# A depthwise convolution ahead of a SwiGLU block: two of the early blocks pass from the token-major to the channel-major convolution, and the convolution's taps are dealt out anew

## The chip, the core and the metric

The program runs on one core of one Trainium2 chip. The core has five engines that each work through their own queue in order: TensorE (PE in the profile, its weight loads PEld), VectorE (DVE), ScalarE (ACT), GpSimd (POOL) and SyncE (SP, which here only issues DMAs). They wait for one another by semaphores. The metric is the device time of one execution in microseconds (us); the median of three executions of the kernel before is 771.72 us (771.16 to 772.36).

## What is computed

`x` has 8 x 4096 tokens of 192 channels. Eight heads of 24 channels each have 7 taps, softmax-normalised; every channel is convolved causally along the sequence with its head's taps. The result goes through a gated feed-forward block of width 1536.

```python
w = weight - np.max(weight, axis=-1, keepdims=True)
w = np.exp(w)
w = w / (np.sum(w, axis=-1, keepdims=True) + 1e-09)
x_pad = np.concatenate([np.zeros((B, pad, D)), x], axis=1)      # pad = 6
out = np.einsum('hk,bskhg->bshg', w, x_unf)                     # 7 shifted copies of x
...
g = x @ w_gate                                                  # 192 -> 1536
silu = g * (1.0 / (1.0 + np.exp(-g)))
val = x @ w_val
return (silu * val @ w_out)                                     # 1536 -> 192
```

## The kernel before

**Blocks and steps.** The 32768 tokens are cut into 64 blocks of 512. A block goes through 12 chunks of 128 of the 1536 hidden columns, so there are 768 steps; step n is chunk j = n mod 12 of block b = n div 12. `gate_val(n)` (line 734) issues, for one step, six matmuls: three slices of 64 channels for the gate and, in the other 64 rows of the array, three for the value, in turn. ScalarE then makes `sig` (silu of the gate) and VectorE `h` = `sig` x value. Gate and value each have three PSUM banks, so the matmuls of step n+3 wait until `sig` and `h` of step n have read theirs.

**Down matmuls.** Behind every third step stands one of four `slot`s: 24 matmuls that multiply six chunks of `h` with the output weights, one half of the rows at a time, into two accumulators (`down`, line 759). In the steady order these are k = 1 behind chunk 7, 2 behind chunk 10, 3 behind chunk 1 of the next block and 4 behind its chunk 4; the last also copies the sums out (ScalarE one half, VectorE the other) and has SP store them. Block 0 has its slots behind steps 9, 12, 15 and 17 (lines 864 to 866). Where a slot changes which half of the rows writes which bank (`swap`), its first matmul is made to wait for a silu (`after`).

**Two ways to the convolved block.** The feed-forward needs each block channel-major, as three tiles `xc[b]` of 128 x 512.

- *Token-major, for the first blocks.* TensorE convolves windows of tokens with a band matrix: `early` for blocks 0 and 1, and `early_pair` (line 379) for blocks 2 and 3 at step 19 and 4 and 5 at step 27: 64 small matmuls into gate and value banks, which ScalarE and VectorE copy to `tme`. From there a block either is turned by TensorE (`eturn`: blocks 0, 1, 2) or goes through DRAM: SP writes it out (`eout`, 4 DMAs) and reads it back by three DMA transposes (`efetch`: blocks 3, 4, 5). The inputs `xp` of the pairs are loaded at the start by GpSimd's DMAs and doubled by SP's (`twice`).
- *Channel-major, for the rest.* Four blocks make a unit; unit 1 here holds blocks 6 and 7 alone (`first_of`). GpSimd's DMA casts the tokens of a unit to fp16 in DRAM (`cast_x`), SP's DMA transposes bring them channel-major into SBUF (`turn_x`, four per two blocks) and a copy joins the last 64 channels of both blocks (`join_x`). Two blocks then are three jobs: a "block" job for 128 channels of each and a "pair" job for the remaining 64 of both. A job (`conv_job`, line 580) has 7 taps: ScalarE multiplies the first into `total` (fp32) and two more into `part` tiles, VectorE adds two taps into `total` (line 618, `tap * x + total`), GpSimd adds the `part`s, and multiplies (line 608, `piece`) and adds (line 593) the last two. All GpSimd's work of a job is issued after VectorE's and ScalarE's taps. `place` (line 653) then has SP move halves of the results into the other two tiles of each block, four DMAs.

**The order.** Each engine's order is the order of issue in the program. `pooled_work(n, j)` (line 708) deals out the taps: behind chunks 1, 7 and 10 one VectorE tap each and one ScalarE tap (two behind chunk 10 of even blocks); one more ScalarE tap stands ahead of the slot of chunk 4. `plan`, filled by `planned(v)` (line 678), holds at which step a unit's cast, transposes and jobs are issued. A block is handed over (`place`) once its two jobs are issued, 14 steps later or 16 steps ahead of its use.

Of the kernel before, what the change touches and what calls it, by code (L numbers as in the profile page):

```python
# [10 lines left out]
def kernel(  # L11
# [172 lines left out]
    xp = {}  # L184
    for e in (2, 4):
        xp[e] = cpool.tile([P, 4 * EG, D], fp16, tag="xp", name="xp")
        for r in range(2):
            windows(xp[e], Q * r, (e + r) * TB, CO, 0, 4 * EG)
        twice(xp[e])

# [243 lines left out]
    def efetch(b):  # L434
        xc[b] = []
        for k in range(SL):
            t = cpool.tile([P, XW], fp16, tag=f"xc{k}", name=f"xc{k}", bufs=8)
            seq(
                nc.sync.dma_start_transpose(
                    out=t[:, 0:TB], in_=scre[b][0:TB, Q * k : Q * k + P]  # L440
                )
            )
            xc[b].append(t)

    def eturn(b, where, then=None):
        c, j = (2, EO) if b < 2 else (4, CO)
        tiles = [
            cpool.tile([P, XW], fp16, tag=f"xc{k}", name=f"xc{k}", bufs=8)
            for k in range(SL)
# [75 lines left out]

    def first_of(u):
        return HALF if u == 1 else 0

    def head_x(u):
        rows = XP + UT - first_of(u) * TB  # L530
        xs[u] = dpool.tile([rows, D], fp16, tag="xs", name="xs")
        if u % upb == 0:
            seq(
                nc.sync.dma_start(
                    out=xs[u].rearrange("t d -> (t d)")[0 : XP * D].rearrange(
                        "(a n) -> a n", n=P
                    ),
                    in_=fill[0 : XP * D // P, :],
                )
            )  # L540

    def cast_x(u):
        t0 = u * UT + first_of(u) * TB
        rows = XP + u * UT + UT - t0
        flat = xs[u].rearrange("t d -> (t d)")
        skip = XP if u % upb == 0 else 0
        n = (rows - skip) * D // P
        seq(
            nc.gpsimd.dma_start(  # L549
                out=flat[skip * D : rows * D].rearrange("(a n) -> a n", n=n),  # L550
                in_=bass.AP(
                    tensor=x_flat.tensor,
                    offset=(t0 - XP + skip) * D,
                    ap=[[n, P], [1, n]],
                ),
                max_dma_last_dim=2048,
            )
        )

    def turn_x(u, i, at):  # L560
        r0 = TB * (i - first_of(u))
        rows = xs[u][r0 : r0 + TB + XP]
        tiles = (x01, x12)[at // Q]
        tag = f"x{at // Q}"
        t = cpool.tile([P, TB + XP], fp16, tag=tag, name=tag, bufs=8)
        seq(nc.sync.dma_start_transpose(out=t, in_=rows[:, at : at + P]))
        tiles[u, i] = t
# [4 lines left out]
    FIRST, ON_DVE = 0, (1, 2)  # L572
    SHARES = ((3, 4), (5, 6)), ((3, 4), (5, 6)), ((3, 4), (5, 6))
    act_steps = []
# [5 lines left out]
    def conv_job(u, what, i):  # L580
        index = n_jobs[0]
        n_jobs[0] += 1
        on_act, on_pool = SHARES[index % len(SHARES)]
        job = {"dve": len(ON_DVE), "act": len(on_act), "parts": []}
        at = XP - pad
# [3 lines left out]

        def add(part, k):  # L590
            total = job["total"]
            seq(
                nc.gpsimd.tensor_tensor(  # L593
                    job["dst"] if k == K - 1 else total, total, part, op=ALU.add
                )
            )

        def proceed():
            if job["dve"]:
                return  # L600
            while job["parts"]:
                add(*job["parts"].pop(0))
            if job["act"]:
                return
            for k in on_pool:
                part = cpool.tile([P, TB], fp32, tag="piece", name="piece", bufs=2)
                seq(
                    nc.gpsimd.tensor_scalar(  # L608
                        part, shifted(k), scalar1=job["tap"][:, k : k + 1],
                        scalar2=1.0, op0=ALU.mult, op1=ALU.mult,  # L610
                    )
                )
                add(part, k)
            finished[u, what, i] = step_now[0]

# [10 lines left out]
        def act_step(k):  # L626
# [12 lines left out]
            else:  # L639
                part = cpool.tile([P, TB], fp32, tag="part", name="part", bufs=8)  # L640
                job["parts"].append((part, k))
            seq(
# [3 lines left out]
            )  # L646
            if k != FIRST:
                job["act"] -= 1
                proceed()

        act_steps.extend((index, lambda k=k: act_step(k)) for k in (FIRST, *on_act))

    def place(u, i):
        b = UB * u + i
        for k in (1, 2):
            xc[b].append(
                cpool.tile([P, XW], fp16, tag=f"pxc{k}", name=f"pxc{k}", bufs=4)
            )
        t0, t1, t2 = xc[b]
        y = y2[u, i // 2][Q * (i % 2) : Q * (i % 2) + Q, :]  # L660
        for dst, src in (
            (t1[0:Q, 0:TB], t0[Q:P, 0:TB]),
            (t1[Q:P, 0:TB], y),
            (t2[0:Q, 0:TB], y),
            (t2[Q:P, 0:TB], t0[0:Q, 0:TB]),
        ):
            seq(nc.sync.dma_start(out=dst, in_=src))

    plan = {}
    placing = []  # L670

    def queue_jobs(u):
        for i in range(first_of(u), UB, 2):
            for job in (("block", i), ("pair", i // 2), ("block", i + 1)):
                conv_job(u, *job)
        placing.extend((u, i) for i in range(first_of(u), UB))

    def planned(v):
        s0 = ustep * v
        turns = [  # L680
            turn
            for i in range(first_of(v), UB, 2)
            for turn in ((i, 0), (i, Q), (i + 1, Q), (i + 1, 0), (i // 2, None))
        ]
        if v == 1:
            head, cast, jobs = 10, 11, 27
            times = (20, 20, 20, 23, 23)
        elif v == 2:
            head, cast, jobs = 10, 12, 40
            times = (32, 33, 34, 35, 37, 38, 39, 40, 41, 43)  # L690
        elif v == 3:
            head, cast, jobs = 56, 56, 56
            times = range(66, 86, 2)
        else:
            head = cast = s0 - (115 if v > 4 else 100)
            jobs = s0 - 89
            first = s0 - (95 if v > 4 else 87)
            times = range(first, first + 20, 2)
        plan.setdefault(head, []).append(lambda: head_x(v))
        plan.setdefault(cast, []).append(lambda: cast_x(v))  # L700
        for m, turn in enumerate(turns):
            def todo(i=turn[0], at=turn[1]):
                join_x(v, i) if at is None else turn_x(v, i, at)

            plan.setdefault(times[m], []).append(todo)
        plan.setdefault(jobs, []).append(lambda: queue_jobs(v))

    def pooled_work(n, j):
        step_now[0] = n
        if j != 4:  # L710
            ready = dve_steps[0][0] if dve_steps else None
            if j in (1, 7, 10) and ready is not None:
                dve_steps.pop(0)[1]()
            for _ in range(2 if j == 10 and n // NCH % 2 == 0 else 1):
                ahead = act_steps[0][0] if act_steps else n_jobs[0]
# [4 lines left out]
        while placing:  # L720
            u, i = placing[0]
            need = (u, "block", i), (u, "pair", i // 2)
            if not all(job in finished for job in need):
                break
            done = max(finished[job] for job in need)
            if n < max(done + 14, ustep * u + NCH * i - 16):
                break
            placing.pop(0)
            place(u, i)

# [71 lines left out]
    def slot(k, b, after=None):  # L802
# [11 lines left out]
        elif k == 3:  # L814
            down(b, [(False, G[2])], 1, after)
            down(b, [(False, G[3])], 1, None)
        else:
            down(b, [(True, G[2]), (True, G[3])], 0, after)
            o_sb = hpool.tile([P, SUBS, D], fp32, tag="o_sb", name="o_sb", bufs=3)
# [33 lines left out]
    make_band()  # L853
    for v in range(1, NU):
        planned(v)

    for n in range(n_steps):
# [4 lines left out]
        elif n == 8:  # L862
            eturn(1, (gate_bank, val_bank))
        elif n in (9, 12, 15, 17):
            k = {9: 1, 12: 2, 15: 3, 17: 4}[n]
            slot(k, 0, silu[n - 1 if k == 4 else n - 2])
        elif j % 3 == 1 and n > 18:
# [5 lines left out]
            slot(k, b - 1 if j < 7 else b, silu[n - 2])  # L873
        if n in (19, 27):
            early_pair(2 if n == 19 else 4)
        elif n == 20:
# [3 lines left out]
        elif n == 22:  # L880
            efetch(3)
        elif n in (28, 29):
            eout(n - 24)
        elif n in (30, 36):
            efetch(4 if n == 30 else 5)
        pooled_work(n, j)
# [44 lines left out]
```

## Time and profile before

| | |
|---|---|
| time, median of three (lowest, highest) | 771.72 us (771.16, 772.36) |
| the profiled execution: time, span of the trace | 771.32 us, 769.5 us |
| TensorE clock granted | 1.000 |
| VectorE / ScalarE / GpSimd busy | 702.5 / 649.1 / 637.8 us |
| VectorE `h` | 768 times, 682 ns mean |
| VectorE taps | 174 times, 1070 ns mean |
| VectorE `o_sb` copies | 63 times, 548 ns mean |
| ScalarE `sig`, taps | 596 ns, 714 ns mean |
| GpSimd products, adds | 918 ns, 1271 to 1419 ns mean |
| SP moves of 64 KB in `place` | 232 |
| first step's matmuls begin at | 8.84 us |

The profile shows one execution. "Busy" is the time in which an engine has an instruction under way, and a busy engine need not be the one that the end waits for: for that, the profile follows the last instruction back through whatever released it. A timeline line gives start and duration in us, the engine, the line of the kernel, the operation, the tiles it writes and reads with their shapes, how many like it follow one another, and in brackets the idle time before it with the instruction that ended it. Matmuls overlap, so two of them may each last 0.38 us and begin 0.04 us apart.

### The profile page before, as it was taken

The numbers are of one execution on the slowest core, as the hardware profiler recorded it, in microseconds if no ns is written. First come the engines' busy times: TensorE is split into PE (matmuls) and PEld (weight loads), VectorE is DVE, ScalarE is ACT, GpSimd is POOL, SyncE is SP. The second block draws the span as 40 slices with busy tenths as digits, with TensorE's granted clock in tenths as the row PEclk, the third lists the DMA queues.
The fourth block names the chain that finished last, engine by engine and source line by source line (L and its number), as shares of the span: only waits on it lengthen the run. The fifth ranks groups of instructions, "written<-read, shape, count | busy, mean of one in ns | idle before, by whom it ended". The sixth has DMA issues, their size and how long they took to land.

```text
span 769.5 us, 27729 instructions
## 1 busy us (share of the span) xinstructions
PE 763.0 (99%) x11041; PEld 616.1 (80%) x11041; DVE 702.5 (91%) x1048; ACT 649.1 (84%) x1114; POOL 637.8 (83%) x570
## 2 busy tenths in 40 slices
PE   8999999999999999999999999999999999999997
PEld 5878888888888888888888888888888888888886
DVE  7789999999999999999999999999999999999875
ACT  6688888888888888888888888888888888888764
POOL 8039899999989898998989989999899998889700
PEclk9999999999999999999999999999999999999999
DMA  9966646653536444456443545447454453121211
GB/s 143 198 115 122 154 80 149 128 88 84 123 81 124 106 85 108 99 95 119 92 102 89 100 111 108 92 82 118 92 120 101 82 116 92 53 70 37 71 56 43
DMA packets 145762, 77.52 MB, mean 101 GB/s; under 512 B 79976, under 2 KB 145504, under 8 KB 145632
## 3 DMA queue, kind: packets, MB, share of 16 engines
q1 hardware_dynamic: 126720, 61.05, 34.3%
q0 software_dynamic: 18912, 14.70, 13.8%
q8 instruction: 86, 1.41, 0.8%
q14 instruction: 44, 0.36, 0.2%
HBM read 29.39 MB, written 37.46 MB: 87 GB/s over the span
## 4 chain that ended last, share of the span: by engine, by line
PE 99%; ACT 0%; DVE 0%; issue 0%
PE val L743 51%; PE acc L769 33%; PE gate L743 14%; PE warm L837 0%; PE turn L457 0%; PE acc L790 0%; PE cv L394 0%; PE cv L350 0%; ACT tme L368 0%; DVE h L754 0%; ACT wide L308 0%; ACT o_sb L899 0%; PE taps L295 0%; DVE spread L275 0%; PE ctap L513 0%
## 5 line engine op out<-in xcount | busy, mean ns | idle before, releaser
L754 DVE TENSOR_TENSOR h<-sig,val 128x512 f16<-128x512 f16 x768 | 497.1, 682 | 59.4 <-PE gate L743 54.3
L752 ACT ACTIVATE sig<-gate 128x512 f16<-128x512 f32 x768 | 457.5, 596 | 107.9 <-PE gate L743 78.3
L743 PE MATMUL gate<-pxc,w 64*128 64x512 f16 x2088 | 488.0, 376 | 0.0
L743 PE MATMUL val<-pxc,w 64*128 64x512 f16 x2088 | 488.0, 376 | 0.0
L743 PEld LDWEIGHTS <-w 64*128 64x128 f16 x4608 | 360.1, 110 | 119.7 <-issue 0.7
L769 PE MATMUL acc<-wo,h 64*128 64x192 f16 x6096 | 336.7, 243 | 0.0
L769 PEld LDWEIGHTS <-h 64*128 64x128 f16 x6096 | 311.6, 94 | 21.4 <-ACT sig L752 0.4
L593 POOL TENSOR_TENSOR total<-total,part 128x512 f32<-128x512 f32 x174 | 221.8, 1275 | 73.8 <-DVE total L618 50.0
L618 DVE SCALAR_TENSOR_TENSOR total<-x,both_taps,total 128x512 f32<-128x512 f16 x174 | 186.2, 1070 | 0.0
L608 POOL TENSOR_SCALAR piece<-x,both_taps 128x512 f32<-128x512 f16 x174 | 159.7, 918 | 0.0
L593 POOL TENSOR_TENSOR total<-total,piece 128x512 f32<-128x512 f32 x87 | 123.5, 1419 | 7.3
L643 ACT ACTIVATE part<-x,both_taps 128x512 f32<-128x512 f16 x174 | 124.3, 714 | 0.0
L593 POOL TENSOR_TENSOR pxc<-total,piece 128x512 f16<-128x512 f32 x58 | 74.2, 1279 | 4.8
L643 ACT ACTIVATE total<-x,both_taps 128x512 f32<-128x512 f16 x87 | 62.1, 714 | 0.0
L743 PE MATMUL gate<-xc,w 64*128 64x512 f16 x216 | 51.4, 377 | 0.0
L743 PE MATMUL val<-xc,w 64*128 64x512 f16 x216 | 51.3, 376 | 0.0
L593 POOL TENSOR_TENSOR y<-total,piece 128x512 f16<-128x512 f32 x29 | 36.8, 1271 | 2.4
L821 DVE COPY o_sb<-acc 128x384 f32<-128x384 f32 x63 | 34.5, 548 | 0.0
L820 ACT COPY o_sb<-acc 128x384 f32<-128x384 f32 x63 | 29.6, 471 | 2.6 <-PE acc L769 2.6
L549 POOL DMA_DIRECT2D xs<-in_x_dram x15 | 11.7, 778 | 0.0
L837 PE MATMUL warm<-fill 128*128 128x512 f16 (+1 forms) x12 | 4.1, 500 | 1.0 <-DVE fill L90 1.0
L470 ACT COPY xc<-turn 128x520 f16<-128x520 f16 (+1 forms) x5 | 2.9, 588 | 1.0 <-PE turn L457 0.9
(66 smaller groups left out, 55.8 us busy)
## 6 DMA issues: line engine op xcount, KB each, us to landing
out_dram<-o_sb SPq DMA_DIRECT2D x63, 384.0 KB
pxc<-pxc SPq DMA_DIRECT2D x116, 64.0 KB
pxc<-y SPq DMA_DIRECT2D x116, 64.0 KB
xs<-in_x_dram POOLq DMA_DIRECT2D x7, 774.0 KB, 8.6
xs<-in_x_dram POOLq DMA_DIRECT2D x7, 768.0 KB, 7.0
x<-x SPq DMA_DIRECT2D x29, 66.0 KB
x<-xs SPq DMA_TRANSPOSE x116
xp<-in_x_dram POOLq DMA_DIRECT2D x4, 240.0 KB, 7.5
```

Source lines behind the costliest of these rows:

```text
L549: nc.gpsimd.dma_start(out=flat[skip * D : rows * D].rearrange("(a n) -> a n", n=n), in_=bass.AP(tensor=x_flat.tensor, offset=(t0 - XP + sk ...
L593: nc.gpsimd.tensor_tensor(job["dst"] if k == K - 1 else total, total, part, op=ALU.add)
L608: nc.gpsimd.tensor_scalar(part, shifted(k), scalar1=job["tap"][:, k : k + 1], scalar2=1.0, op0=ALU.mult, op1=ALU.mult,)
L618: nc.vector.scalar_tensor_tensor(job["total"], shifted(k), job["tap"][:, k : k + 1], job["total"], op0=ALU.mult, op1=ALU.add,)
L643: nc.scalar.activation(part, shifted(k), AF.Copy, scale=job["tap"][:, k : k + 1])
L743: nc.tensor.matmul(o, w16[m][p0 : p0 + Q, k, e::E], xc[b][k][p0 : p0 + Q, 0:TB], start=(k == 0), stop=(k == SL - 1),)
L752: silu[n] = seq(nc.scalar.activation(sg, g, AF.Silu)).ins
L754: seq(nc.vector.tensor_tensor(hj, sg, v, op=ALU.mult))
L769: nc.tensor.matmul(acc[b][bank][:, s, :], hj[p0 : p0 + Q, ts(2 * bank + s, P)], wo16[p0 : p0 + Q, j, :], start=(not second and j == 0 and ...
L820: seq(nc.scalar.copy(o_sb[:, 0:2, :], acc[b][0]))
L821: seq(nc.vector.tensor_copy(o_sb[:, 2:4, :], acc[b][1]))
L837: nc.tensor.matmul(warm[:, 0:width], fill, fill.unsqueeze(1).to_broadcast([P, width // P, P]), start=True, stop=True, skip_group_check=True,)
```

## The change

Blocks 4 and 5 leave the token-major way. The second `early_pair`, its loads, its trip through DRAM (`eout`, `efetch`) are gone, and unit 1 now holds all of blocks 4 to 7, in two parts with a cast each (`part_of`). The first job's first ScalarE tap is issued inside step 19, ahead of the remaining `early_pair`; it gives one ScalarE tap to GpSimd (`LEAD`).

GpSimd's work of a job is issued earlier: its products as soon as the first ScalarE tap is issued, summed in a tile `rest` of their own; each ScalarE `part` is added to `rest`, and one last add joins `total` and `rest`. There are now four `part` buffers instead of eight.

VectorE's taps: one behind chunk 1, two behind chunk 7, and one behind chunk 10 only for the first two jobs. Results are handed over in parts, each four steps after its job is issued: a "block" result's two moves and a "pair" result's two per block (`place`).

Unit 2's cast moves from step 12 to 38, its transposes from 32..43 to 57..68 and its jobs from 40 to 57; unit 3 follows with its cast at 62 and jobs at 82. Block 0's third slot moves from step 15 to 14 and keeps the second's bank order, so that it needs no wait; its fourth waits for the silu of two steps before rather than one.

```diff
-    for e in (2, 4):
-        xp[e] = cpool.tile([P, 4 * EG, D], fp16, tag="xp", name="xp")
-        for r in range(2):
-            windows(xp[e], Q * r, (e + r) * TB, CO, 0, 4 * EG)
-        twice(xp[e])
+    xp[2] = cpool.tile([P, 4 * EG, D], fp16, tag="xp", name="xp", bufs=1)
+    for r in range(2):
+        windows(xp[2], Q * r, (2 + r) * TB, CO, 0, 4 * EG)
+    twice(xp[2])
...
-    SHARES = ((3, 4), (5, 6)), ((3, 4), (5, 6)), ((3, 4), (5, 6))
+    LEAD, REST = ((3,), (5, 6, 4)), ((3, 4), (5, 6))
+    soon = 2
...
+        def add(to, one, two):
+            seq(nc.gpsimd.tensor_tensor(to, one, two, op=ALU.add))
+
+        def product(k):
+            tag = "rest" if k == on_pool[0] else "piece"
+            part = cpool.tile([P, TB], fp32, tag=tag, name=tag, bufs=2)
+            seq(
+                nc.gpsimd.tensor_scalar(
+                    part, shifted(k), scalar1=job["tap"][:, k : k + 1],
+                    scalar2=1.0, op0=ALU.mult, op1=ALU.mult,
+                )
+            )
+            return part
 
         def proceed():
-            if job["dve"]:
-                return
-            while job["parts"]:
-                add(*job["parts"].pop(0))
-            if job["act"]:
-                return
-            for k in on_pool:
-                part = cpool.tile([P, TB], fp32, tag="piece", name="piece", bufs=2)
...
-                add(part, k)
-            finished[u, what, i] = step_now[0]
+            if job["dve"] == 0 and job["act"] == 0:
+                add(job["dst"], job["total"], job["rest"])
+                finished[u, what, i] = step_now[0]
...
-            if k != FIRST:
-                job["act"] -= 1
-                proceed()
+            if k == FIRST:
+                job["rest"] = product(on_pool[0])
+                for k in on_pool[1:]:
+                    add(job["rest"], job["rest"], product(k))
+                return
+            add(job["rest"], job["rest"], part)
+            job["act"] -= 1
+            proceed()
...
+        if what == "block":
+            t0 = xc[b][0]
+            xc[b] += sides[b]
+            moves = (t1[0:Q], t0[Q:P]), (t2[Q:P], t0[0:Q])
+        else:
+            y = y2[u, i // 2][Q * (i % 2) : Q * (i % 2) + Q, :]
+            moves = (t1[Q:P], y), (t2[0:Q], y)
+        for dst, src in moves:
+            seq(nc.sync.dma_start(out=dst[:, 0:TB], in_=src[:, 0:TB]))
...
-        if v == 1:
-            head, cast, jobs = 10, 11, 27
-            times = (20, 20, 20, 23, 23)
+        if v == 1 and i0 == 0:
+            head, cast, jobs = 10, 11, 18
+            times = (16, 16, 16, 18, 19)
+        elif v == 1:
+            head, cast, jobs = 10, 20, 35
+            times = (30, 30, 31, 33, 34)
         elif v == 2:
-            head, cast, jobs = 10, 12, 40
-            times = (32, 33, 34, 35, 37, 38, 39, 40, 41, 43)
+            head, cast, jobs = 10, 38, 57
+            times = (57, 58, 59, 60, 61, 64, 65, 66, 67, 68)
         elif v == 3:
-            head, cast, jobs = 56, 56, 56
-            times = range(66, 86, 2)
+            head, cast, jobs = 62, 62, 82
+            times = range(74, 94, 2)
...
-        if j != 4:
-            ready = dve_steps[0][0] if dve_steps else None
-            if j in (1, 7, 10) and ready is not None:
+        ready = dve_steps[0][0] if dve_steps else None
+        if ready is not None and n != 19:
+            count = {1: 1, 7: 2, 10: ready < soon}.get(j, 0)
+            for _ in range(min(count, len(dve_steps))):
                 dve_steps.pop(0)[1]()
-            for _ in range(2 if j == 10 and n // NCH % 2 == 0 else 1):
+        if j != 4 and n != 19:
+            many = (j == 10 and n // NCH % 2 == 0) or (
+                act_steps and act_steps[0][0] < soon and j != 1
+            )
+            for _ in range(2 if many else 1):
...
-            done = max(finished[job] for job in need)
-            if n < max(done + 14, ustep * u + NCH * i - 16):
+            done = finished.get((u, what, i if what == "block" else i // 2))
+            if done is None or n < done + 4:
                 break
...
-        elif n in (9, 12, 15, 17):
-            k = {9: 1, 12: 2, 15: 3, 17: 4}[n]
-            slot(k, 0, silu[n - 1 if k == 4 else n - 2])
+        elif n in (9, 12, 14, 17):
+            k = {9: 1, 12: 2, 14: 3, 17: 4}[n]
+            slot(k, 0, None if k == 3 else silu[n - 2])
...
-        if n in (19, 27):
-            early_pair(2 if n == 19 else 4)
+        if n == 19:
+            act_steps.pop(0)[1]()
+            early_pair(2)
...
-        elif n in (28, 29):
-            eout(n - 24)
-        elif n in (30, 36):
-            efetch(4 if n == 30 else 5)
```

## The prediction

> **What bounds the kernel now.** I read the page's busy times first, then the chain that ended last, then the costliest groups, and from there the timelines of the engines in two places: the start, and one stretch of the middle.
>
> ```profile
> PE 763.0 (99%) x11041; PEld 616.1 (80%) x11041; DVE 702.5 (91%) x1048; ACT 649.1 (84%) x1114; POOL 637.8 (83%) x570
> ...
> PE 99%; ACT 0%; DVE 0%; issue 0%
> ...
> L754 DVE TENSOR_TENSOR h<-sig,val 128x512 f16<-128x512 f16 x768 | 497.1, 682 | 59.4 <-PE gate L743 54.3
> L593 POOL TENSOR_TENSOR total<-total,part 128x512 f32<-128x512 f32 x174 | 221.8, 1275 | 73.8 <-DVE total L618 50.0
> L618 DVE SCALAR_TENSOR_TENSOR total<-x,both_taps,total 128x512 f32<-128x512 f16 x174 | 186.2, 1070 | 0.0
> L608 POOL TENSOR_SCALAR piece<-x,both_taps 128x512 f32<-128x512 f16 x174 | 159.7, 918 | 0.0
> ```
>
> TensorE carries 99% of the chain. In the middle it runs three steps and one group of 24 down matmuls in 2.93 us without a break (gates that open a step after such a group: 243.45, 246.38, 249.31). So nothing can be won there, only lost; a gain must come from TensorE's work or gaps near the start:
>
> ```profile
> 25.36 0.38 PE L743 MATMUL val<-xc,w 64*128 64x512 f16 x1
> 25.65 1.16 PE L769 MATMUL acc<-wo,h 64*128 64x192 f16 x24
> ...
> 37.99 0.38 PE L743 MATMUL val<-xc,w 64*128 64x512 f16 x1
> 38.30 0.46 PE L394 MATMUL cv<-xp,band 64*32 64x120 f16 x33
> 39.00 0.40 PE L394 MATMUL cv<-xp,band 64*32 64x120 f16 x31 [0.24 <-DVE h L754]
> 39.33 0.40 PE L743 MATMUL gate<-xc,w 64*128 64x512 f16 x1
> ```
>
> The second `early_pair` (blocks 4, 5) stands between two steps; ahead of block 0's last down group there are 0.29 us from val to acc where 0.09 is usual (23.08 to 23.17).
>
> What matters for the rest is how near VectorE comes to holding TensorE:
>
> ```profile
> 238.32 1.70 DVE L618 SCALAR_TENSOR_TENSOR total<-x,both_taps,total 128x512 f32<-128x512 f16 x1
> 239.95 0.67 DVE L754 TENSOR_TENSOR h<-sig,val 128x512 f16<-128x512 f16 x1
> 240.69 0.38 PE L743 MATMUL val<-pxc,w 64*128 64x512 f16 x1
> ...
> 244.88 2.62 POOL L593 TENSOR_TENSOR total<-total,part 128x512 f32<-128x512 f32 x2 [0.92 <-ACT sig L752]
> 244.92 1.98 DVE L754 TENSOR_TENSOR h<-sig,val 128x512 f16<-128x512 f16 x3 [0.19 <-PE gate L743]
> 246.82 1.23 DVE L618 SCALAR_TENSOR_TENSOR total<-x,both_taps,total 128x512 f32<-128x512 f16 x1
> 255.62 0.75 DVE L618 SCALAR_TENSOR_TENSOR total<-x,both_taps,total 128x512 f32<-128x512 f16 x1
> 255.76 1.73 POOL L593 TENSOR_TENSOR total<-total,piece 128x512 f32<-128x512 f32 x1
> ```
>
> A tap alone takes 0.75. One that begins while GpSimd adds takes until that add's end and 0.55 more (add over at 247.50, tap at 246.82+1.23 = 248.05). An add that begins during a tap ends 1.12 to 1.13 after it (257.49 against 256.37). The two share something that one holds at a time. The 1.70 tap is the worst case: its h ends at 240.62, and the val that reuses the bank starts at 240.69. At the start, where VectorE did hold TensorE, a val follows the h by 0.05 (h 10.37+0.69, val 11.11), so 0.02 was left.
>
> **The change, part by part.**
>
> *Removed, TensorE.* Steps 27 to 28 are 1.90 us apart at their gates against 0.65 elsewhere, and step 28 with its down group takes 1.77 against 1.63: 1.25+0.14 = 1.39 for the second `early_pair`. The down group at 17 now waits for the silu of step 15, not 16: steps 17 and 18 are 1.85 apart against 1.64 where a group stands between elsewhere, so 0.21 go. Moving the third group from 15 to 14 only reorders the same matmuls. Gain 1.60.
>
> *Removed, other engines.* Two ScalarE casts (0.56), two VectorE casts (0.65) and copies (0.25), two GpSimd loads, and on SP two copies, eight stores and six transposes. None is on the chain: nothing.
>
> *Added: three jobs (90, not 87).* ScalarE 9 x 0.714 = 6.4, VectorE 6 x 1.07 = 6.4, GpSimd 3 x 7.1 = 21.2 (2 x 1.275 + 1.419 + 1.28 + 2 x 0.918 = 7.08 each; the first trades a ScalarE tap for a GpSimd product). Cover: GpSimd sits idle 29.3 us before its first add at 48.34. Then a job comes every 8 steps, 7.82 us, so 7.08 fits. Without that cover block 4 would be late at step 48, which starts at 59.35-1.60 = 57.8. By program order its last part is issued at step 31 and moved at 35; step 31 starts at about 41, its taps end near 45, the add near 47, the move (landing 2 to 3 after issue by the semaphores) near 51. Nothing, with 6 us over. Later blocks have 13 steps, 12.7 us, from move to use.
>
> *First tap inside step 19.* ScalarE's tap (0.71) stands ahead of `early_pair`'s casts, in the 0.80 that ScalarE waited before 29.54 (0.2 earlier now). Its tile must land by about 28.6. The 390 KB cast was issued at 17.73 and landed 10.5 later, 28.2. Two loads fewer stand before it; by the semaphores the last two xp loads landed 2.5 after the second, so 25.7, and a transpose lands 2.6 after issue: 28.3. If only the 1.4 us of issuing is saved, it is 29.5 and costs 0.9. I take 0. Behind this wait stand two casts and the silu of step 20.
>
> *SP and the second cast.* SP gets four transposes, a join and eight moves for what it loses. GpSimd's added cast (390 KB, blocks 6 and 7) is issued behind its first five products and adds, near 33; at the 7.0 of the 768 KB casts it lands at 40, and SP asks at about 41, after block 1's store. At 10.5 it would be 44; three transposes, the join and another transpose (near 9 us with one landing) then put the last moves for block 4 near 56, still under 57.8. Hand-overs go in two halves four steps after issue. A move waits on GpSimd's last add, and behind it in SP stand the next transposes and an output store; by the pass below it waits under 1 us, and what waits has over 10 us. Unit 2's transposes from step 57 serve taps from step 61. ScalarE may now wait for GpSimd, with four `part` buffers instead of eight; at two parts a job that is two jobs of lead, and the pass uses each part within one. Nothing each.
>
> *VectorE's taps.* Three per block stay, but none behind chunk 10 and two in a row behind chunk 7. Let R be the gate of chunk 8 after the down group (246.38 in the lines). Chunk 7's h ends at R+0.52 (246.90), the next VectorE instruction starts at R+0.44. Chunk 11's val starts at R+2.93+0.18 = R+3.11 (gate 249.31, val 249.49) and needs chunk 8's h, 0.67 long, over 0.05 before, so begun by R+2.39. An instruction starts 0.08 before its forerunner's end, so two taps may sum to 2.39-0.44+0.16 = 2.11. The 1.70 tap agrees: its R was 237.59, its h began at R+2.36.
>
> Pairs of taps are of two kinds, in turn. Both of a "pair" job: GpSimd then has nothing but that job's last add, so 0.75+0.04+0.75: fits. Last tap of a block and first of the next: here I follow GpSimd from the former pair (t = 0 at its first tap; add 1.27, product 0.69, 0.08 between dependent ones, 0.14 after VectorE). Second tap ends 1.53; last add 1.67-2.94; products to 3.61 and 4.29; adds 4.37-5.64, 5.72-6.99; the single tap of chunk 1 comes at 5.87, so it ends 6.99+0.55 = 7.54; add 7.07 to 7.54+1.13 = 8.67; products to 9.34, 10.02; adds 10.10-11.37, 11.45-12.72. At 11.73 the next pair begins: first tap 0.99+0.55 = 1.54, second 0.75, sum 2.29, over by 0.18. This recurs every 24 steps, at 43, 67 ... 715: 29 times, 5.2 us. From nothing (add over 0.2 sooner) to 1.82+0.75-2.11 = 0.46 each, 13.3 in all. I take 0.18, since each row repeats to 0.02.
>
> The Trainium skill, "SBUF — State Buffer", section "SBUF: two separate sides", says that VectorE and GpSimd share a port pair under an exclusive lock held for the whole instruction. The rows agree on the exclusion, but a tap needs only 0.55 after the add, not its whole 0.75. By the rule's letter the first tap would be 1.74, the stall 0.38, and the time 781.1 (an estimate); the rows decide.
>
> Sum: -1.60 + 5.2 = +3.6. The profiled execution took 771.32, 1.8 around its span of 769.5; the median of three, 771.72, is 0.4 above it. The span becomes 773.1, the median 775.3.
>
> **The rivals.**
>
> *The taps fit.* GpSimd's pass is 0.2 us quicker over its ten instructions, and only the gain is left: 771.72-1.60 = 770.1. For: 0.2 in 11 is little, and no row shows two taps in a row. Against: the pass is built of rows that repeat.
>
> *The other order.* The single tap comes 0.14 after the add of 5.72. If it comes first, it takes 0.75 (to 6.61), the adds run to 7.74 and 9.09, the products to 10.45, an add to 11.80; the first of the two taps takes 0.75, the next add starts in it, and the second tap stands behind that add: 1.13+0.55. Sum about 2.49, 0.38 over, 29 times: 11.0, so 781.1. It decides from 0.14 us of slip on. Against: in the lines the order of a 23.46 us pattern never flips.
>
> *The early tile is late.* Step 19 costs 0.9: 771.0 without the stalls above, 776.2 with them.
>
> **How the numbers follow.** Stalls near 0.18: 0.65, own range 773.0 to 778.5 (0.10 to 0.29 each). Taps fit: 0.21, 769.9 to 770.8, with or without a little of the tile. Other order: 0.10. Late tile alone: 0.04. The measurement can tell about 0.2%, 1.5 us, from no change: below 770.2 is faster, above 773.3 slower. Taps fit splits 0.13 to 0.08; the tile and the low end of the stalls add 0.09 to no change; slower 0.70. The range reaches from 770.0 to 779.5 and leaves out the other order and a sliver below.
>
> **What would show it.** No cv matmuls between steps 27 and 28, step 48 some 1.6 us earlier. In the middle, gates 23.46 us apart over 24 steps become 23.64, the extra ahead of chunk 11's val in every second block, with "DVE h" as the releaser; taps in the pattern 0.75, 0.75, 1.67, 1.54, 0.75. Wrong if the 24 steps still take 23.46, if two taps in a row interleave with a GpSimd add, or if TensorE waits for a DMA at steps 48 or 60.

## The result, and the profile after it

| | before | after |
|---|---|---|
| median, lowest to highest, runs on the same chip | 771.62 us, 771.16 to 772.36, 4 | 782.94 us, 780.43 to 783.42, 4 |
| ratio of the times, 95% interval | | 1.0139, 1.0116 to 1.0162 |
| profiled execution: time, span | 771.32, 769.5 | 783.08, 781.1 |
| first step's matmuls begin at | 8.84 | 9.22 |

The change made the kernel 11.3 us slower, 1.4%. The page of the profile after, busy times, chain and groups, in the order in which the prediction read them:

```profile
span 781.1 us, 27597 instructions
...
PE 768.8 (98%) x10977; PEld 617.6 (79%) x10977; DVE 721.4 (92%) x1050; ACT 652.1 (83%) x1120; POOL 624.2 (80%) x588
...
PE 95%; DMA 2%; SPq 1%; POOL 0%; ACT 0%; DVE 0%; issue 0%; POOLq 0%; DVEq 0%
...
L758 PE MATMUL gate<-pxc,w 64*128 64x512 f16 x2160 | 510.2, 377 | 3.7 <-DMA pxc<-pxc 3.7
...
L613 DVE SCALAR_TENSOR_TENSOR total<-x,both_taps,total 128x512 f32<-128x512 f16 x180 | 209.2, 1175 | 1.1
```

TensorE carried 99% of the chain before; now 2% of it is DMA and 1% SP, and a gate waits 3.7 us for `pxc<-pxc`, one of `place`'s moves. A mean VectorE tap takes 1175 ns instead of 1070. These are two separate losses. Where each falls is seen from the starts of the gates: in the steady state a step takes 0.649 us, or 1.634 with a down group behind it. What a step takes beyond that is called lost from here on. Summed up:

| where | before | after | difference |
|---|---|---|---|
| first matmul's start | 8.84 | 9.22 | +0.38 |
| steps 0 to 47, without the stall at 47 | 5.57 | 3.80 | -1.77 |
| steps 47 and 71, ahead of chunk 11's val | 0 | 0.91 + 0.89 | +1.80 |
| step 84, late moves | 0 | 1.40 | +1.40 |
| step 108, late moves | 0 | 4.37 | +4.37 |
| steps 109 and 110, slower matmuls | 0 | 1.38 + 0.32 | +1.70 |
| steps 143, 167 ... 719, ahead of chunk 11's val | 0 | 25 x 0.156 | +3.89 |

This comes to 11.8, by which the last step's gate starts later (774.34 against 762.50); the two profiled executions differ by as much (783.08 - 771.32 = 11.76).

**The late moves.** The timelines of GpSimd, SP and TensorE around step 84 of the changed kernel, and under them two pieces of its chain of waits (start, length, what):

```profile
78.46 4.23 SPq L567 DMA_TRANSPOSE x<-xs  x3
78.76 0.82 POOL L549 DMA_DIRECT2D xs<-in_x_dram  x1
90.61 0.46 SPq L571 DMA_DIRECT2D x<-x  x1
92.48 1.17 SPq L670 DMA_DIRECT2D pxc<-pxc  x2
97.00 0.38 PE L758 MATMUL val<-pxc,w 64*128 64x512 f16 x1 [1.24 <-DMA pxc<-pxc]
```
```profile
81.11 9.42 DMA x<-xs
...
93.06 3.90 DMA pxc<-pxc
```

GpSimd issues unit 3's cast (L549) at 78.76, in the middle of SP's three transposes of unit 2 (L567). By the semaphores the cast lands at 90.4, and the three transposes, which land 2.7 us after issue at the median, take 7.0, 8.7 and 9.4. The join (L571) has to wait for them, so SP stands from 82.69 to 90.61. The two moves of block 7 (L670) stand in SP's queue behind it, are issued at 92.48, and TensorE waits for the second at 97.00. The same happens at step 108: unit 4's cast is issued at 108.69, a transpose at 110.57 lands 9.1 us later, the join starts at 119.75, the moves at 122.23, and TensorE, idle for 3.73 us, starts at 124.13:

```profile
108.69 0.76 POOL L549 DMA_DIRECT2D xs<-in_x_dram  x1
110.57 1.81 SPq L567 DMA_TRANSPOSE x<-xs  x1
119.75 0.47 SPq L571 DMA_DIRECT2D x<-x  x1
122.23 1.11 SPq L670 DMA_DIRECT2D pxc<-pxc  x2
124.13 0.37 PE L758 MATMUL gate<-pxc,w 64*128 64x512 f16 x1 [3.73 <-DMA pxc<-pxc]
```

**VectorE's pairs.** GpSimd, VectorE and TensorE around step 143:

```profile
157.68 1.27 POOL L593 TENSOR_TENSOR rest<-rest,part 128x512 f32<-128x512 f32 x1
157.96 2.20 DVE L613 SCALAR_TENSOR_TENSOR total<-x,both_taps,total 128x512 f32<-128x512 f16 x2
160.46 0.38 PE L758 MATMUL gate<-pxc,w 64*128 64x512 f16 x1
160.81 0.37 PE L758 MATMUL val<-pxc,w 64*128 64x512 f16 x1
```

The first of two taps (1.54) waits for the add that is under way, the second takes 0.75, and chunk 11's val follows its gate by 0.35 instead of 0.18: 0.17 lost. This is the picture that the prediction drew.

### The profile page after: what moved, and what is told of

The parts are those of the page before. It is cut to its first block, busy times and chain, and to the rows that moved or that the text cites. A ratio compares the mean times of both kernels' runs of the same rounds, so it can differ in the third digit from the quotient of the medians.

```text
span 781.1 us, 27597 instructions
## 1 busy us (share of the span) xinstructions
PE 768.8 (98%) x10977; PEld 617.6 (79%) x10977; DVE 721.4 (92%) x1050; ACT 652.1 (83%) x1120; POOL 624.2 (80%) x588
## 4 chain that ended last, share of the span: by engine, by line
PE 95%; DMA 2%; SPq 1%; POOL 0%; ACT 0%; DVE 0%; issue 0%; POOLq 0%; DVEq 0%
PE val L758 48%; PE acc L784 32%; PE gate L758 14%; DMA x<-xs 1%; DMA pxc<-pxc 1%; PE warm L854 1%; SPq L567 0%; PE turn L456 0%; DVE total L613 0%; PE acc L805 0%; POOL y L593 0%; POOL rest L593 0%; ACT sig L767 0%; PE cv L349 0%; SPq L670 0%
## 5 line engine op out<-in xcount | busy, mean ns | idle before, releaser
L758 PE MATMUL gate<-pxc,w 64*128 64x512 f16 x2160 | 510.2, 377 | 3.7 <-DMA pxc<-pxc 3.7
L758 PE MATMUL val<-pxc,w 64*128 64x512 f16 x2160 | 506.0, 376 | 2.1 <-DMA pxc<-pxc 1.2
L593 POOL TENSOR_TENSOR rest<-rest,part 128x512 f32<-128x512 f32 x179 | 237.2, 1325 | 15.1 <-ACT part L637 6.0
L613 DVE SCALAR_TENSOR_TENSOR total<-x,both_taps,total 128x512 f32<-128x512 f16 x180 | 209.2, 1175 | 1.1
L593 POOL TENSOR_TENSOR pxc<-total,rest 128x512 f16<-128x512 f32 x60 | 87.5, 1458 | 45.4 <-PE val L758 22.8
L593 POOL TENSOR_TENSOR rest<-rest,piece 128x512 f32<-128x512 f32 x91 | 116.3, 1278 | 7.6
L593 POOL TENSOR_TENSOR y<-total,rest 128x512 f16<-128x512 f32 x30 | 38.2, 1273 | 45.8 <-DVE total L613 28.3
L599 POOL TENSOR_SCALAR rest<-x,both_taps 128x512 f32<-128x512 f16 x90 | 62.6, 696 | 10.0 <-DMA x<-xs 10.0
L599 POOL TENSOR_SCALAR piece<-x,both_taps 128x512 f32<-128x512 f16 x91 | 62.8, 690 | 0.0
L758 PE MATMUL val<-xc,w 64*128 64x512 f16 x144 | 34.3, 376 | 0.7 <-DVE h L769 0.7
L549 POOL DMA_DIRECT2D xs<-in_x_dram x16 | 12.4, 775 | 0.0
```

The source lines that it names most:

```text
L549: nc.gpsimd.dma_start(out=flat[skip * D : rows * D].rearrange("(a n) -> a n", n=n), in_=bass.AP(tensor=x_flat.tensor, offset=(t0 - XP + sk ...
L593: seq(nc.gpsimd.tensor_tensor(to, one, two, op=ALU.add))
L599: nc.gpsimd.tensor_scalar(part, shifted(k), scalar1=job["tap"][:, k : k + 1], scalar2=1.0, op0=ALU.mult, op1=ALU.mult,)
L613: nc.vector.scalar_tensor_tensor(job["total"], shifted(k), job["tap"][:, k : k + 1], job["total"], op0=ALU.mult, op1=ALU.add,)
L758: nc.tensor.matmul(o, w16[m][p0 : p0 + Q, k, e::E], xc[b][k][p0 : p0 + Q, 0:TB], start=(k == 0), stop=(k == SL - 1),)
```

## The experiments

The theory was that two things are wrong, and that they add: casts that fly beside SP's transposes, and two taps in a row. Each kernel below is the changed one with the lines shown, but for one that starts from the kernel before. The kernel before took 771.48 (13 runs), 771.49 (17) and 771.64 (21) in the three groups of runs.

**Casts moved off the transposes.** Unit 3's cast goes 16 steps earlier, unit 4's from step 92 to 95.

```diff
-            head, cast, jobs = 62, 62, 82
+            head, cast, jobs = 46, 46, 82
-            head = cast = s0 - (115 if v > 4 else 100)
+            head = cast = s0 - (115 if v > 4 else 97)
```

> Unit 3's cast is issued at step 46 instead of 62 and unit 4's at 95 instead of 92, so that neither lies beside the DMA transposes that feed blocks 7 and 9; nothing else differs. Theory (the casts hold the transposes up, and SP stands behind the join that waits for them): the losses ahead of steps 84 and 108 in the changed kernel, 1.4 + 4.4 us, go, and with them 1.7 us of steps that ran slower just after the second; the time falls by about 7.5 us, to 775.4. Rival (moving results by halves four steps after issue is too late in itself): the losses stay, 783. The 25 losses of 0.15 us behind pairs of VectorE taps stay with both. The loss of 0.9 us at step 67, where the cast was issued beside the taps, should fall to 0.2 to 0.4; that at step 43 stays.

Measured: 776.31 us (775.84 to 777.13, 4 runs), ratio 1.0063 (1.0046 to 1.0080). No stop at 84, and at 108 0.47 instead of 4.37, with no slower steps after it. The 0.92 at 47 and 0.15 every 24 steps stayed; the 0.89 at 71 fell to 0.14. The rest at 108 is my own making: at 95 unit 4's cast was issued at 111.22, ahead of the moves of 115.21, the second of which landed only at 119.98. In this profile 0.78 more was lost at step 21 as well, long before the edit has an effect; no other trace shows it.

**Taps one by one.**

```diff
-            count = {1: 1, 7: 2, 10: ready < soon}.get(j, 0)
+            count = {1: 1, 7: 1, 10: 1}.get(j, 0)
```

> VectorE's taps are dealt out as before the change, one behind each of chunks 1, 7 and 10; the casts stay. Theory: the 25 losses of 0.15 us and both of 0.9 us go, 5.6 us in all, while the DMA waits at steps 84 and 108 stay: 777.3. Rival (the small losses come of GpSimd's new order, not of two taps in a row): they stay in size and number, 783.

Measured: 776.74 us (774.78 to 777.58, 4 runs), ratio 1.0065 (1.0049 to 1.0081). No loss is left from step 111 to the end: 240 steps take 234.6 us, as before. The two losses of 0.9 at 47 and 71 went too. The stops at 84 (1.74) and 108 (3.72 and 1.70 behind it) stayed. So the pairs make the small losses that recur, and the two large ones do not need them.

**Both.**

> Both edits: casts at 46 and 95, one tap behind each of chunks 1, 7 and 10. If the two causes are all there is and add up, only the gain of 1.6 us at the start is left: 770.0 to 770.4, below the kernel before. If there is a third cause, it stays above 771.6.

Measured: 772.11 us median, ratio 1.0011 (1.0001 to 1.0021); ten runs spread from 771.1 to 774.6. That is above the forecast. The profiled execution was the fastest (771.11); even there 0.26 was lost at step 49 and 0.74 at step 108, where unit 4's cast (108.65) again flies beside the moves (112.0). That this is what varies from run to run is likely: the kernels with a stop of 3.5 us or more at 108 also spread over 2.8 to 3.8 us, the kernel before over 1.1 to 1.9. It is not shown, as each kernel has a trace of one run only, and the kernels with the casts far ahead, below, still spread over 0.9 to 2.5.

**Unit 3's cast alone**, at 46; unit 4's stays at 92 as in the change.

> Unit 3's cast alone is moved, to step 46. Theory: the loss ahead of step 84 goes (1.4 us), that ahead of step 108 stays at 4 us or so, since it belongs to unit 4's cast: about 781. If both go, one late transfer caused both; if both stay, the casts are not the cause.

Measured: 775.0 us in one run. Against my expectation both stops went. The timelines of GpSimd and SP show why:

```profile
62.51 0.82 POOL L549 DMA_DIRECT2D xs<-in_x_dram  x1
78.61 3.98 SPq L567 DMA_TRANSPOSE x<-xs  x3
84.14 0.46 SPq L571 DMA_DIRECT2D x<-x  x1
...
104.17 1.36 SPq L567 DMA_TRANSPOSE x<-xs  x1
107.10 0.76 POOL L549 DMA_DIRECT2D xs<-in_x_dram  x1
107.38 0.48 SPq L571 DMA_DIRECT2D x<-x  x1
```

With unit 3's cast at 62.51 the three transposes land by 84.06, and the join follows 6.5 us sooner than in the change. At step 108 unit 4's cast was still where the change has it, but now it was issued 2.9 us after the transpose that the join needs, which landed at 107.32. The moves for block 9, issued at 109.86 and 110.38, then flew beside the cast for 6.8 and 6.5 us and landed by 116.9, ahead of step 108 at 117.64. The order of two queues that nothing ties together decides.

**Unit 3's cast and the taps one by one.** If that order is a matter of a microsecond, another deal of VectorE's taps, which moves both queues a little, may turn it over.

> Unit 3's cast at step 46 alone (unit 4's stays at 92, as in the change), and one VectorE tap behind each of chunks 1, 7 and 10. Theory: as the run with unit 3's cast alone (775.0), without its 25 stalls of 0.155 (3.9 us) and without the 0.9 at step 47: 770.2 us, no stop at 84 or 108. Rival (the order of taps sets how late unit 4's moves are, as in the run with both edits): a stop of 0.7 or more at step 108, 771 to 772.

Measured: 776.74 us (773.84 to 777.65, 6 runs), ratio 1.0063 (1.0050 to 1.0076). The rival held, and by far more than it claimed. GpSimd, SP and TensorE around step 108:

```profile
105.86 0.76 POOL L549 DMA_DIRECT2D xs<-in_x_dram  x1
107.03 1.95 SPq L567 DMA_TRANSPOSE x<-xs  x1
116.48 0.48 SPq L571 DMA_DIRECT2D x<-x  x1
...
120.87 0.37 PE L758 MATMUL gate<-pxc,w 64*128 64x512 f16 x1 [3.08 <-DMA pxc<-pxc]
```

Here the cast (105.86) is 1.2 us ahead of the transpose (107.03), which lands 9.4 us later; the join and the moves slip as in the change, and 5.0 us go. Against the run before, the cast came 1.2 us sooner and the transpose 2.9 later. This pair of runs is the clearest for the cause: the cast stands at step 92 in both, and no DMA is edited between them; VectorE's taps are, and with them the order of cast and transpose. The first of the pair is one run alone.

**Casts far ahead, taps one by one.** Unit 3's cast at 46, unit 4's at 72.

```diff
-            head = cast = s0 - (115 if v > 4 else 100)
+            head = cast = s0 - (115 if v > 4 else 120)
```

> Unit 3's cast at step 46 instead of 62, every later unit's cast 120 steps ahead of its first step (unit 4: 72) instead of 100 (92), so that no cast flies while SP's transposes are asked for; VectorE's taps one behind each of chunks 1, 7 and 10. Theory (the change's loss is made of moves held up by a cast in flight at steps 84 and 108, and of two taps in a row behind chunk 7): nothing of either is left, TensorE's 24 steps take 23.46 us from step 48 on, and only the gain of 1.6 to 1.8 us at the start stays: 769.9 to 770.3 us against 771.5 before. Rival (what was left in the run with both edits, 0.26 at step 49 and 0.74 at step 108, is no matter of unit 4's cast): 771 to 772 again, with a stop at step 108.

Measured: 770.76 us (770.16 to 772.63, 11 runs), ratio 0.9992 (0.9984 to 1.0001). From step 65 on nothing is lost to the end. At the start 1.7 are gained, and given back are 0.28 at 49, where a down group waits for an `h` behind a tap that an add held up (1.42 instead of 0.75), and 0.51 at 64, where ScalarE waits 1.4 us for unit 2's transpose that flies beside unit 3's cast (62.51, landing 72.1). My forecast of 769.9 to 770.3 overlooked these two.

**Unit 3's cast earlier still**, at 40 and at 44; the rest as in the run before.

> As the run with the casts at 46 and 72 and the taps one each (770.8 us, profile with 0.28 lost at step 49 and 0.51 at step 64, where ScalarE waits 1.37 us for unit 2's first transpose, issued 4.6 us after unit 3's cast): unit 3's cast at step 40, right behind unit 2's, so that GpSimd issues it near 57 instead of 62.5. Theory (a transpose lands late only while a cast is in flight): the cast lands by 67 to 70, the transposes of 67.1 and 69.1 sooner, the 0.51 at step 64 goes: 770.2 us. Rival (two casts in a row take the DMA engines as long, and now hold up the moves of 58 too): 0.5 or more again, at 60 or 64: 770.8 or more.

> The same with unit 3's cast at step 44 (GpSimd issues it near 59.5, behind the move of 58): the 0.51 at step 64 shrinks or goes, nothing else changes: 770.2 to 770.6 us by the theory, 770.8 by the rival.

Measured: 770.57 us (770.01 to 772.40, 11 runs), ratio 0.9987 (0.9978 to 0.9996), and 770.60 (770.21 to 771.08, 11 runs), ratio 0.9986 (0.9977 to 0.9995). The 0.51 at step 64 went, as the theory has it, but 0.72 and 1.24 came at step 48. The timelines of the first of the two:

```profile
54.12 2.46 SPq L670 DMA_DIRECT2D pxc<-y  x4
54.34 0.76 POOL L549 DMA_DIRECT2D xs<-in_x_dram  x1
...
59.48 0.37 PE L758 MATMUL gate<-pxc,w 64*128 64x512 f16 x1 [0.45 <-DMA pxc<-y]
```

These are block 4's moves. The first, issued ahead of unit 2's cast, landed after 2.2 us, the second, issued behind it, after 4.7. In the run with the cast at 46 both were ahead (53.21 and 53.79, the cast at 54.22) and landed after 2.3 and 2.1. In the run with the cast at 44 the cast (53.69) was again ahead of the second move (54.07), which landed after 5.3. It is the same race once more, lost by 0.4 us, and the program does not settle it. These are still the best kernels of the study: 1.0 us, 0.13 to 0.14%, under the kernel before. Both intervals lie below 1, but the gain is less than the 0.2% which the prediction took as its bound for a difference.

**Why 0.9 at step 47.** In the changed kernel the pair of taps at step 43 took 2.93, far over the 1.54 and 0.75 of the later pairs. The timelines of the kernel with unit 3's cast alone show it too:

```profile
54.24 0.76 POOL L549 DMA_DIRECT2D xs<-in_x_dram  x1
54.57 2.95 DVE L613 SCALAR_TENSOR_TENSOR total<-x,both_taps,total 128x512 f32<-128x512 f16 x2
55.02 1.28 POOL L593 TENSOR_TENSOR rest<-rest,part 128x512 f32<-128x512 f32 x1
```

No add is under way when the first tap begins, only GpSimd's issue of unit 2's cast. Yet the add that starts 0.45 later runs unhindered in 1.28, to 56.30, and the tap ends 0.56 behind it, at 56.86. So the tap was held off by the issue, and the add behind it went first. The test issues that cast two steps earlier:

```diff
-            head, cast, jobs = 10, 38, 57
+            head, cast, jobs = 10, 36, 57
```

> As the run with unit 3's cast alone at step 46 (775.0 us), and unit 2's cast issued at step 36 instead of 38: GpSimd then issues this DMA (0.76 us) well ahead of the pair of taps of step 43, not just ahead of it. Theory (GpSimd's issue of a cast holds VectorE's tap off, and the add behind it goes first again): the loss of 0.92 us ahead of chunk 11 of step 47 falls to between 0 and 0.7, and the first tap of that pair no longer ends 0.55 after an add that began behind the issue. Rival (the issue has no part in it): 0.92 again. The rest as there, 774 to 775 us.

Measured: 775.6 us in one run. The issue came at 51.75, with no tap beside it; the first tap took 1.03, held by an add that was under way, and the loss at step 47 fell from 0.92 to 0.68. What remains is the order in which the second tap stands behind a waiting add (1.75). At step 48 0.63 were lost anew, to block 4's moves beside the cast. The theory's range held, but it was wide. A second sign is step 71 of the first experiment: with unit 3's cast gone from beside its pair, 0.89 became 0.14. That an issue always holds a tap off is not so, as the last section shows.

**The pairs without the rest of the change.** The kernel before, with VectorE's taps alone dealt as in the change:

```diff
-            if j in (1, 7, 10) and ready is not None:
+            for _ in range(min({1: 1, 7: 2}.get(j, 0), len(dve_steps))):
                 dve_steps.pop(0)[1]()
```

> The kernel before with VectorE's taps alone dealt as in the change (one behind chunk 1, two behind chunk 7, none behind chunk 10); GpSimd keeps its old order, products after the adds, all behind the last tap of a job. Theory (two taps in a row meet GpSimd's adds whatever their order, and a second tap that stands behind an add costs 1.68 us): a stall of near 0.4 us in every second block, some 27 times, 10 us in all: near 782 us, 24 steps in 23.85 us. Rival (the pair costs only under GpSimd's new order): 771.5 as before, 24 steps in 23.46 us.

Measured: 782.08 us (781.73 to 782.32, 4 runs), ratio 1.0137 (1.0122 to 1.0152). From step 95 on 0.40 are lost in every 24 steps, 27 times, 10.8 in all; nothing else is lost from there on. VectorE, GpSimd and TensorE in one of them:

```profile
246.15 2.43 DVE L618 SCALAR_TENSOR_TENSOR total<-x,both_taps,total 128x512 f32<-128x512 f16 x2
246.22 1.81 POOL L593 TENSOR_TENSOR total<-total,piece 128x512 f32<-128x512 f32 x1
...
249.23 0.37 PE L743 MATMUL val<-pxc,w 64*128 64x512 f16 x1 [0.21 <-DVE h L754]
```

The add begins in the first tap, ends 1.13 after it, and the second tap 0.55 after that: 0.75 + 1.13 + 0.55 = 2.43. This is the order of the prediction's second rival, which the changed kernel itself never settled into. So a pair costs under GpSimd's old order too, and there 0.40 instead of 0.156.

## Why the prediction was wrong, step by step

It forecast 775.3 us and a range of 770.0 to 779.5. The direction was right; the forecast was 7.6 us short of the measured 782.94, which lies 3.4 us above the range.

*Gain at the start, 1.60.* Right: 1.77. No cv matmuls stand between steps 27 and 28, and the early tile was not late, as step 19 lost nothing new.

*Three more jobs on GpSimd, nothing.* Right: step 48, the first of block 4, lost nothing.

*VectorE's pairs, 0.18 each, 29 times.* The mechanism and the recurrence were right: 0.156 each, 25 times, 3.9 us. With the first tap's 1.54 and the two taps' limit of 2.11 it is also seen that the waiting rule read from single taps carries over to pairs. Two of the 29 were sized wrong: steps 47 and 71 lost 0.9 each, since at 54.48 and 78.76 GpSimd issued a cast beside the pair, and this issue was put at nothing in the pass. Two did not occur, at 95 and 119, behind the two stops.

*The step that failed* is "SP and the second cast". It says "Unit 2's transposes from step 57 serve taps from step 61", that a move "waits under 1 us, and what waits has over 10 us", and closes with "Nothing each." I gave every transpose its landing of 2.6 us from the kernel before and weighed the delays inside SP's queue only. I did not lay GpSimd's queue beside it. Unit 3's cast went from step 56 to 62, into unit 2's transposes of 57 to 68; in the kernel before no transpose is issued while a cast is in flight, since the next ones read what that cast writes (cast at 71.78, landed by the semaphores at 81.20, next transpose at 81.22):

```profile
71.78 0.84 POOL L549 DMA_DIRECT2D xs<-in_x_dram  x1
73.21 0.47 SPq L667 DMA_DIRECT2D pxc<-pxc  x1
81.22 1.93 SPq L566 DMA_TRANSPOSE x<-xs  x1
```

What waits behind a late transpose is not a tap with time to spare but the join, and in SP's order the moves of a block that TensorE needs next. The price was 1.40 at 84 and 4.37 at 108, and the slower clock behind the second, 1.70: 7.5 of the 8.0 us by which the forecast of the span (773.1) fell short of 781.1. The rest, to within 0.2, is the 0.9s at 47 and 71 (+1.4), the smaller and absent stalls (-1.0), the gain (-0.2) and the later first matmul (+0.4).

The prediction named "TensorE waits for a DMA at steps 48 or 60" as what would make it wrong. The sign was right, the place was not: the waits came at blocks 7 and 9. None of its rivals had a place for a cast.

The Trainium skill, "DMA: Bandwidth & Descriptors", section "Queues, rings and completion order", says that each DMA engine goes round-robin between the queue rows with work, a packet at a time. The traces agree in kind: in the changed kernel the four transposes issued within 4 us behind a cast landed after 6.7 to 9.4 us, the other 116 after 2.74 at the median (the two issued just ahead of a cast, at 78.46 and 108.64, after 7.0 and 6.9). None of the traces shows the round itself, and that page gives no time for a transpose with a cast in flight. But the trace of the kernel before had a near price, in `place`'s 64 KB moves: the eight that were issued 1.4 to 3.6 us behind the casts of 71.78 and 111.60 landed, by the semaphores, after 6.8 to 8.4 us (that of 73.21 above after 8.3), those with no cast in flight after 2.05 at the median. The prediction's "landing 2 to 3 after issue" passed over these eight. No step waited for them there, so they cost nothing and did not show in the chain.

## What to carry to other kernels

When a transfer's issue is moved, lay the other engines' DMA queues beside it over the whole flight of the largest transfer, and ask what stands behind the first waiting instruction on the same queue. A race between two queues that no semaphore ties together can be decided anew by an edit that shifts either engine: another deal of VectorE's taps, which has nothing to do with DMA, came with 5 us lost. Two instructions in a row on an engine that shares a lock lose the slack that lies between single ones: a single tap of 1.70 cost nothing in the kernel before, pairs of 2.20 and 2.43 cost 0.17 and 0.40.

## What the runs showed of the hardware beyond that

**An idle gap and the granted clock.** After TensorE's idle 3.73 us at step 108 the first matmuls take 0.38 as ever, but from 125.1 on they take 0.63, for some 3.4 us. The windows of the changed kernel, with PE's, PEld's, DVE's, ACT's and POOL's busy time, then the granted clock:

```profile
124.00:128.00 4.00, 3.73 (x34) 2.77 (x35) 1.86 (x3) 1.80 (x3) 3.62 (x4) 0.64 0.73 191
128.00:132.00 4.00, 4.00 (x55) 3.13 (x53) 2.58 (x5) 2.80 (x6) 0.32 (x1) 0.94 0.36 76
125.20:128.40 3.20, 3.20 (x34) 2.74 (x31) 2.12 (x3) 1.36 (x3) 2.42 (x3) 0.50 0.66 164
128.60:131.50 2.90, 2.90 (x44) 2.36 (x42) 1.83 (x3) 2.36 (x5) 0.00 (x0) 1.00 0.31 64
```

The clock is 0.64 on average in the first; it is 0.50 from 125.2 to 128.4, and back from 128.6. Behind the 1.24 us at step 84 it stays at 1.00, and the run that lost 5.0 us at 108 shows 0.50 from 121.3 to 124.5, behind 3.08 us of idle time. So the waits of 3.08 and 3.73 us had a price beyond their length, in the changed kernel 1.70 on top of 4.37, and the one of 1.24 had none; where between them it begins, no run shows. The Trainium skill, "TensorE: Matmul & The Clock Gate", section "What's actually happening", puts the gate's window at some 3.4 us of idle time. The slow stretch here is as long as that window, but 3.08 us of idle time was enough to bring it on.

**GpSimd's issue of a DMA and VectorE's taps.** In all twelve traces together, the six taps that begin 0.33 to 0.43 us into the 0.76 or 0.82 of such an issue were held up; in the two that had no add behind the issue the tap took 0.97 instead of 0.75. The 42 taps that begin 0.15 to 0.18 into it, the 72 that begin 0.66 or more into it, and the one at 0.46 were not. In the changed kernel:

```profile
193.33 0.76 POOL L549 DMA_DIRECT2D xs<-in_x_dram  x1
193.50 1.53 DVE L613 SCALAR_TENSOR_TENSOR total<-x,both_taps,total 128x512 f32<-128x512 f16 x2
```

Both taps take 0.75 there. What of the issue holds a tap off, and from when to when, the traces do not show.

**The first matmul** begins between 8.8 and 9.6 us in kernels whose code up to there is the same. That is 0.8 us between traces, nearly as much as the last edits were worth. Each kernel has one trace, so whether it differs by kernel or by run is not shown.
